# Decoding the packed weights on two engines: the low bits on GpSimd, the combining on VectorE

## The chip, the cores and the metric

The kernel runs on one core of a Trainium2 chip. The core has five engines with a queue of instructions each: TensorE (PE, matmuls), VectorE (DVE), ScalarE (ACT), GpSimd (POOL) and SyncE (SP, which here issues the loads and the transposes by DMA). The metric is the device time of one execution in microseconds, as the median of several runs; lower is better.

## The reference

Attention with a mask from hashed buckets, then a feed-forward layer with an ELU over its output:

```python
q_bits = (einsum('bhsd,dk->bhsk', q, proj) > 0)          # 6 bits a row, k the same
mask = q_bucket[:, :, :, None] == k_bucket[:, :, None, :]
scores = where(mask, q @ k.T / sqrt(D), -1e9)
attn = softmax(scores) ;  x = attn @ v                   # B 4, H 8, S 768, D 64
h = x @ w_in                                             # 3072 x 512 by 512 x 2048
g = where(h > 0, h, exp(min(h, 0)) - 1)
out = g @ w_out                                          # 3072 x 2048 by 2048 x 512
```

q, k, v and proj come as 32-bit numbers. The weights `w_in` and `w_out` come as 64-bit floating-point numbers, and the kernel reads them as pairs of 32-bit words.

## The kernel before, in words

**Work.** A batch has 8 heads, taken as 4 pairs. A chunk is a batch's rows that go through the feed-forward layer together: 2 x 128 tokens (three chunks) for the first batch, 3 x 128 (two chunks) for each other one. For each chunk and pair of heads the attention is done in steps called duos, each of two tiles of 128 rows: scores on PE (line 831), the row maximum while the scores leave PSUM on DVE (line 845), the exponential on ACT (line 869), then the normalised probabilities as two halves of 16 bits each, high part on ACT (`a_scaled`, line 238) and rest on DVE (`v_rest`, line 256), then a transpose by DMA (line 901) and the product with v on PE (line 924). When all four pairs of a chunk are done, its feed-forward matmuls can run (`h`, line 1002; `o`, line 1061), with the ELU between them on ACT, POOL (line 1027) and DVE (line 1030). Every matmul operand is split in this way into a high part and a rest of 16 bits, so each product is three matmuls.

**The weights.** `w_part` brings in 32 slabs of 128 x 512 weights, 16 of `w_in` and 16 of `w_out`. For each slab `load` (line 726) moves the 64-bit numbers into one of three places of a ring in the tile `U` (token `w`), or, for some of the slabs, into a spare place inside the tile `W` (token `raw`). Each number is a low and a high 32-bit word, next to each other. `prelu` on ACT (line 743) reads the high words and makes a 32-bit float from them whose last three bits have still to come. `shift` on DVE (line 747) shifts the dense slab left by three bits in place. `tail` on DVE (line 751) shifts the low words right by 29 and joins them in. Then the place in the ring is free again. `bound` on PE (line 762) sums the squares of the slab for the common scale. When 16 slabs are through, `scale` makes the scale of that matrix, and then each slab is split: `hi` on POOL (`scaled`, line 244) and `lo` on DVE (`v_rest`, line 256).

**The order.** Every step is a job with an engine, an estimated duration, a key (a due time counted in duos), the jobs it comes after, and tokens for buffers that it takes and gives back. `run_plan` simulates the engines with these estimates and with the constants at the head of the file (`HOP`, the delay from one engine to another; `BANK_HOP`, `LATE`, `LEAD`, `V_LEAD`, `W_KEY`, `OFF`), and emits the instructions in the order that it finds. On the chip each engine keeps the order of its own queue and waits where an input is not ready. `W_KEY` sets the keys of the weights: decoding at `W_KEY[0] + W_KEY[1] * i`, loads earlier by `W_KEY[2]` (a negative number: later), the splits of `w_in` from `W_KEY[3]` in steps of `W_KEY[4]`, those of `w_out` from `W_KEY[5]` in steps of `W_KEY[6]`. The jobs of the feed-forward layer on PE have keys over 1000, so PE takes them when nothing of the attention is due. `OFF` gives the key offset of each attention step. `GP` names the engine of some of the elementwise steps.

Of the kernel before, what the change touches and what calls it, by code (L numbers as in the profile page):

```python
# [49 lines left out]
GP = {'w': 'POOL', 'v0': 'ACT', 'v': 'POOL', 'k0': 'ACT', 'k': 'ACT', 'q0': 'POOL', 'q': 'ACT', 'kd': 'DVE', 'qd': 'DVE', 'kd0': 'POOL', 'qd0': 'DVE', 'ld': 'POOL', 'ld0': 'POOL'}  # L50
LATE_BITS = ()
FIRST = ((0,), (1,), (2,), (3,))
OUT = ("ACT", "DVE", "ACT")
OFF = {"S": -3.7, "M": -2.5, "N": 2.5, "E": 2.4, "R": -2.1, "H": 0.1, "L": -1.5, "A": 0.1}


@with_exitstack
def lsh_attention_moe(
# [10 lines left out]
    nc = tc.nc  # L69
# [459 lines left out]

    def bits_late(st, tag, key, after, w, quads, ways, dst, which):  # L530
        box = {}

        def mm():
            t = ps_a.tile([P, 512], F32, tag="av", name="z")[:, :w]
            box["t"] = t
            for n, (zi, src, rows) in enumerate(ways):
                for u in range(quads):
                    nc.tensor.matmul(  # L538
                        t[u * QD : (u + 1) * QD], pj["z"][:rows, zi, :], flat(st[src])[:rows, u * w : (u + 1) * w],
                        start=n == 0, stop=n == len(ways) - 1,  # L540
                    )

        def cmp():
            zb = small.tile([P, HALF], F16, tag="zb", name="zb", bufs=2)[:, :w]
            box["zb"] = zb
            used = slice(0, quads * QD)
            nc.vector.tensor_scalar(  # L547
                zb[used], box["t"][used], pj["thr"][used, which : which + 1], (MBIT, -MBIT)[which], ALU.is_gt, ALU.mult
            )

        def send():
            for u in range(quads):
                nc.sync.dma_start(flat(st[dst])[D : D + 2 * NB, u * w : (u + 1) * w], box["zb"][u * QD : u * QD + 2 * NB])

        m = job("PE", 0.08 + 0.22 * len(ways) * w / HALF, mm, key, after=after, take=("av",), kind="z")
        c = job("DVE", 0.13 + w * 0.00105, cmp, key, after=(m,), take=("zb",), give=("av",))
        return job("SP", 0.78 * quads, send, key, after=(c,), give=("zb",), move=0.1, lanes=quads)

    def q_split(ns, ps, nt, sgs, keys, early, made, klos):
        sts = [qs[n] for n in ns]  # L560
        w = len(ns)
        for i, (n, p, st, sg) in enumerate(zip(ns, ps, sts, sgs)):
# [19 lines left out]

            ky = keys[2] + (1.0 * i if not early else 0.0)
# [124 lines left out]
    def w_part():  # L708
        wst["acc"] = ps_o.tile([P, 512], F32, tag="o2", name="acc")[:, :SL]
        raw_users = []  # L710
        before = None
        decoded = {}
        scales = {}
        products = None
        for i in range(NSI + NSO):
# [28 lines left out]

            def shift(d=d):
                di = d.bitcast(I32)
                nc.vector.tensor_scalar(di, di, 3, None, ALU.logical_shift_left)  # L747

            def tail(i=i, d=d):
                di = d.bitcast(I32)  # L750
                nc.vector.scalar_tensor_tensor(di, w64.pop(i)[:, :, 0], 29, di, ALU.logical_shift_right, ALU.bitwise_or)  # L751

# [17 lines left out]
            if is_raw:  # L770
                raw_users.append(j3)
            decoded[i] = j3
            products = job("PE", 0.4, bound, key, after=(j3,), behind=(products,))
            if last:

                def scale(o=o):
                    nc.vector.tensor_reduce(wst["m2"][:, o : o + 1], wst["acc"], axis=AX.X, op=ALU.max)
                    wst["ex", o], wst["sc", o] = powers(
                        wst["m2"][:, o : o + 1], 1, 2.0**-34, W_TOP, f"w{o}", const, squares=True
                    )  # L780
                    if o == 1:
# [3 lines left out]
                scales[o] = products = job("DVE", 1.5, scale, key, after=(products,), take=("av",), give=("av",))  # L785
# [21 lines left out]
    def pair_part(n, ci, b, p, c0, nt, key0):  # L807
# [8 lines left out]
        for d, duo in enumerate(duos):  # L816
# [70 lines left out]
            for i, at in enumerate(duo):  # L887
# [300 lines left out]
```

## Time and profile before

| | |
|---|---|
| median of 3 runs | 886.24 us (885.35 to 886.65) |
| profiled execution: its own time | 886.83 us |
| profiled execution: span, first to last instruction | 884.7 us |
| mean granted TensorE clock | 0.964 |
| busy: PE, DVE, ACT, POOL | 804.8, 705.4, 664.6, 207.4 us |
| line 747, `shift`: count, mean | 32, 433 ns |
| line 751, `tail`: count, mean | 24 from the ring, 683 ns; 8 from `W`, 802 ns |
| line 743, `prelu`: count, mean | 24 and 8, 660 ns |

Busy time is the time in which an engine works on an instruction; waiting is not in it. A row of operations names the line, the engine, the operation, the tiles written and read, the shapes and the count, then the total and mean time. Where a line is that of a helper (238, 244, 256), the tiles tell the caller.

### The profile page before, as it was taken

How to read it: one execution, taken by the hardware profiler on the slowest of the kernel's cores; microseconds unless marked ns; L12 is line 12 of the kernel's file. 1: busy time of each engine (PE TensorE's matmuls, PEld its weight loads, DVE VectorE, ACT ScalarE, POOL GpSimd, SP SyncE). 2: the span in 40 equal slices, each digit the busy share in tenths (PEclk: the TensorE clock that was granted, in tenths of full speed). 3: DMA queues.
4: the chain of work that ended last, by engine and by line, in shares of the span. 5: the costliest groups of instructions: out<-in, count | busy, mean ns of one | idle time of the engine just before them, and what ended most of it. 6: DMA issues, size and time to landing. Idle time of an engine off the chain costs nothing.

```text
span 884.7 us, 15645 instructions
## 1 busy us (share of the span) xinstructions
PE 804.8 (91%) x5425; PEld 450.8 (51%) x5425; DVE 705.4 (80%) x1470; ACT 664.6 (75%) x1300; POOL 207.4 (23%) x268
## 2 busy tenths in 40 slices
PE   4666469999999987999999999999999999999996
PEld 2333246656666644555554555555555555555553
DVE  6999999999888777899796887898888868772321
ACT  7978457889697879987886888988778877862331
POOL 2100634422312101133131212142222112121211
PEclk9977579999999999999999999999999999999999
DMA  8588985999697889886897989987868786760000
GB/s 299 162 232 231 216 206 117 155 188 183 153 184 148 138 165 214 173 144 144 156 183 120 162 175 177 187 162 165 160 136 150 140 129 121 151 116 18 37 1 36
DMA packets 394927, 135.72 MB, mean 153 GB/s; under 512 B 370464, under 2 KB 389216, under 8 KB 394848
## 3 DMA queue, kind: packets, MB, share of 16 engines
q1 hardware_dynamic: 392768, 128.43, 72.1%
q0 software_dynamic: 1920, 6.29, 2.1%
q8 instruction: 42, 0.69, 0.3%
q14 instruction: 37, 0.30, 0.1%
q10 hardware_dynamic: 160, 0.00, 0.0%
HBM read 35.65 MB, written 6.29 MB: 47 GB/s over the span
## 4 chain that ended last, share of the span: by engine, by line
PE 62%; DVE 16%; issue 7%; ACT 5%; DMA 5%; SPq 2%; POOL 2%; POOLq 0%; DVEq 0%; ACTq 0%
PE o L1061 22%; PE h L1002 22%; PE ss L831 9%; PE av L924 7%; DVE hl L256 4%; DVE pt L845 4%; DVE W L256 1%; DVE W L751 1%; PE z L538 1%; ACT pt L869 1%; DVE U L1030 1%; DMA kst<-in_k_dram 1%; ACT hl L238 1%; DMA qst<-in_q_dram 1%; DVE W L747 1%
## 5 line engine op out<-in xcount | busy, mean ns | idle before, releaser
L1002 PE MATMUL h<-x,W 128*128 128x384 f16 (+1 forms) x1728 | 280.5, 309 | 1.1 <-DVE U L1030 1.1
L1061 PE MATMUL o<-W,U 128*128 128x512 f16 x1152 | 280.2, 383 | 0.4 <-ACT U L238 0.4
L256 DVE SCALAR_TENSOR_TENSOR hl<-pt,duo,hl 128x768 f16<-128x768 f32 x192 | 197.1, 1032 | 27.5 <-ACT hl L238 26.5
L1002 PEld LDWEIGHTS <-W 128*128 128x128 f16 x1728 | 167.1, 98 | 98.3 <-issue 7.7
L1027 POOL TENSOR_SCALAR U<-U,ch 128x384 f32<-128x384 f32 (+1 forms) x120 | 110.2, 918 | 434.6 <-ACT U L1023 316.6
L238 ACT ACTIVATE hl<-pt,duo 128x768 f16<-128x768 f32 x192 | 175.7, 925 | 33.5 <-DVE duo L882 28.4
L845 DVE TENSOR_SCALAR_CACHE_REDUCE pt<-ss 128x768 f32<-128x768 f32 x184 | 174.4, 948 | 32.7 <-PE ss L831 30.8
L869 ACT ACTIVATE pt<-pt,duo,sg 128x768 f32<-128x768 f32 x192 | 195.6, 1019 | 2.3
L1061 PEld LDWEIGHTS <-U 128*128 128x128 f16 x1152 | 111.4, 98 | 123.3 <-issue 9.0
L831 PE MATMUL ss<-K,O 128*128 128x384 f16 x736 | 154.6, 333 | 10.9 <-DVE pt L845 10.3
L831 PEld LDWEIGHTS <-O 128*128 128x128 f16 (+1 forms) x768 | 72.6, 100 | 78.1 <-issue 29.8
L924 PE MATMUL av<-PT,vhl 128*64 128x384 f16 (+1 forms) x1296 | 106.9, 322 | 5.1 <-DMA PT<-hl 3.2
L1023 ACT ACTIVATE U<-h,ch 128x384 f32<-128x384 f32 (+1 forms) x120 | 71.1, 592 | 49.1 <-PE h L1002 48.9
L238 ACT ACTIVATE U<-U,ch 128x384 f16<-128x384 f32 (+1 forms) x120 | 75.5, 629 | 38.8 <-PE o L1061 33.6
L1030 DVE SCALAR_TENSOR_TENSOR U<-h,U 128x384 f32<-128x384 f32 (+1 forms) x120 | 69.0, 575 | 41.3 <-POOL U L1027 41.2
L256 DVE SCALAR_TENSOR_TENSOR U<-U,ch 128x384 f16<-128x384 f32 (+1 forms) x120 | 77.6, 646 | 22.5 <-ACT U L238 22.1
L924 PEld LDWEIGHTS <-vhl 128*64 128x64 f16 x1296 | 74.3, 115 | 37.9 <-issue 12.0
L861 ACT ACTIVATE duo<-duo,sg 128x2 f32<-128x2 f32 x96 | 27.6, 287 | 30.0 <-DVE pt L845 29.6
L248 POOL COPY nat2q<-nat2q 128x192 f32<-128x192 f32 (+1 forms) x34 | 22.0, 646 | 119.2 <-DVE nat2q L256 84.5
L762 PE MATMUL acc<-W 128*128 128x128 bf16 x128 | 16.3, 264 | 27.2 <-DVE W L751 26.9
L869 ACT ACTIVATION_READ_ACCUMULATOR pt<-pt,duo,sg 128x1 f32 x192 | 36.0, 187 | 0.0
L547 DVE TENSOR_SCALAR zb<-z,pjt 64x384 f16<-64x384 f32 (+2 forms) x44 | 25.5, 579 | 6.5 <-PE z L538 6.1
(124 smaller groups left out, 571.0 us busy)
## 6 DMA issues: line engine op xcount, KB each, us to landing
U<-in_moe_w_in_dram SPq DMA_DIRECT2D x12, 512.0 KB
vf<-in_v_dram SPq DMA_DIRECT2D x16, 384.0 KB
U<-in_moe_w_out_dram SPq DMA_DIRECT2D x12, 512.0 KB
out_dram<-W POOLq DMA_DIRECT2D x24, 256.0 KB, 4.0
kst<-in_k_dram SPq DMA_DIRECT2D x14, 384.0 KB
qst<-in_q_dram SPq DMA_DIRECT2D x24, 192.0 KB
PT<-hl SPq DMA_TRANSPOSE x192
W<-in_moe_w_in_dram SPq DMA_DIRECT2D x4, 512.0 KB
```

The costliest lines, as they stand in the source:

```text
L238: nc.scalar.activation(o, x, AF.Copy, scale=s)
L256: nc.vector.scalar_tensor_tensor(o, x, s, hi, ALU.mult, ALU.subtract)
L831: nc.tensor.matmul(t[:, x, :HALF], st[o][:rows, at, :], kst[kk][:rows, j * NC + x * HC : j * NC + (x + 1) * HC, :].rearrange("p a b -> p ( ...
L845: nc.vector.tensor_scalar(pt.rearrange("p (n e) -> p n e", n=2), box["s", i][:, :, :HALF], CLAMP, None, ALU.max, ALU.max, accum_out=box["d ...
L861: nc.scalar.activation(u[:, 2:4], u[:, 0:2], AF.Copy, scale=st["sg"][:, 1:2])
L869: nc.scalar.activation(pt, pt, AF.Exp, bias=u[:, 2 + i : 3 + i], scale=st["sg"][:, 0:1], accum_out=u[:, 4 + i : 5 + i])
L924: nc.tensor.matmul(av[j * D : (j + 1) * D], vst["v"][p][:, j, c, vx, :], PTs[j][:, :nt, px, c, :], start=n_ == 0 and c == 0, stop=n_ == 2 ...
L1002: nc.tensor.matmul(box["h"][:, x * w : (x + 1) * w], WH[:, g * KT + t, wx, fc * P : (fc + 1) * P], xs[ns[t]][:, xx, :], start=x == 0 and t ...
L1023: nc.scalar.activation(box["e"], box["h"], AF.Exp, scale=css[b][:, 0:1])
L1027: nc.gpsimd.tensor_scalar(box["e"], box["e"], css[b][:, 2:3], css[b][:, 3:4], ALU.mult, ALU.add)
L1030: nc.vector.scalar_tensor_tensor(box["e"], box["h"], 0.0, box["e"], ALU.max, ALU.min)
L1061: nc.tensor.matmul(banks[bank][:, :DO], box["g"][:, gx, at : at + P], WH[:, NSI + f, wx, :], start=f == 0 and i == 0, stop=f == NF - 1 and ...
```

## The change

`prelu` stays. The new `shift` runs on GpSimd: it takes the low words as unsigned integers, multiplies them by 2^-29, takes the minimum with 7 and writes the result, rounded to an integer, over the low words. It no longer reads what `prelu` writes, so both wait for the load alone. `tail` on VectorE shifts the dense slab left by three bits and joins the low words in, in one instruction. It waits for `prelu` and for `shift`. The instruction on VectorE that only shifted is gone.

With it the plan gets new numbers: estimated durations of some steps, hops, leads, weight keys and offsets. The load of a slab into the ring is tied in the plan to the `tail` that frees its place.

```diff
-HOP = {"PE": 0.00, "ACT": 0.50, "DVE": 0.20, "POOL": 0.39, "SP": 0.49}
+HOP = {"PE": 0.00, "ACT": 0.50, "DVE": 0.20, "POOL": 0.20, "SP": 0.49}
-BANK_HOP = {"s0": 0.58, "s1": 0.58, "h": 0.00, "av": 0.00, "PT": 0.52, "hl": 1.44}
+BANK_HOP = {"s0": 0.58, "s1": 0.58, "h": 0.14, "av": 0.00, "PT": 0.52, "hl": 1.44}
-V_LEAD = (8.8, 7.7, 8.8, 2.9)
-V_LEAD0 = (-2.2, -1.0, 1.7, 1.5)
-W_KEY = (-4.6, 0.39, -1.3, 6.8, 0.20, 13.0, 0.33)
+V_LEAD = (7.4, 7.7, 8.8, 2.9)
+V_LEAD0 = (-2.2, -1.2, 4.4, 1.5)
+W_KEY = (-4.6, 0.39, -1.9, 5.8, 0.20, 14.4, 0.12)
-GP = {..., 'ld0': 'POOL'}
+GP = {..., 'ld0': 'POOL', 'sh': 'POOL'}
+WPE = 0
+JOINT = False
-OFF = {"S": -3.7, "M": -2.5, "N": 2.5, "E": 2.4, "R": -2.1, "H": 0.1, "L": -1.5, "A": 0.1}
+OFF = {"S": -3.2, "M": -2.5, "N": 2.5, "E": 2.5, "R": -2.1, "H": -0.6, "L": -1.5, "A": 0.1}
...
-            before = job("SP", 0.45, load, key - W_KEY[2], behind=(before,), take=ring, move=1.7)
+            last_use = staged[-3] if not is_raw and len(staged) > 2 else None
+            before = job("SP", 0.45, load, key - W_KEY[2], after=(last_use,), behind=(before,), take=ring, move=1.7)
...
-            def shift(d=d):
-                di = d.bitcast(I32)
-                nc.vector.tensor_scalar(di, di, 3, None, ALU.logical_shift_left)
+            apart = GP["sh"] == "POOL"
+
+            def shift(i=i, d=d):
+                if apart:
+                    low = w64[i][:, :, 0]
+                    nc.gpsimd.tensor_scalar(low, low.bitcast(U32), 2.0**-29, 7.0, ALU.mult, ALU.min)
...
             def tail(i=i, d=d):
                 di = d.bitcast(I32)
-                nc.vector.scalar_tensor_tensor(di, w64.pop(i)[:, :, 0], 29, di, ALU.logical_shift_right, ALU.bitwise_or)
+                low = w64.pop(i)[:, :, 0]
+                if apart:
+                    nc.vector.scalar_tensor_tensor(di, di, 3, low, ALU.logical_shift_left, ALU.bitwise_or)
...
             j1 = job("ACT", 0.56, prelu, key, after=wait)
-            j2 = job("DVE", 0.34, shift, key, after=(j1,))
-            j3 = job("DVE", 0.6, tail, key, after=(j2,), give=ring)
+            if apart:
+                j2 = job("POOL", 1.15, shift, key, after=wait)
...
+            j3 = job("DVE", 0.72 if is_raw else 0.62, tail, key, after=(j1, j2), give=ring)
...
-            w_ready[i] = job("DVE", 0.66, lo, key, after=(h,))
+            if i >= WPE:
+                w_ready[i] = job("DVE", 0.74, lo, key, after=(h,))
...
-                l = job("DVE", 0.93, lo, kd + OFF["L"], after=(h,), behind=los, give=("pt",) + (("duo",) if i == 1 else ()))
+                l = job("DVE", 0.95, lo, kd + OFF["L"], after=(h,), behind=los, give=("pt",) + (("duo",) if i == 1 else ()))
```

The plan's estimate for the copies of q on POOL (`dup`, `dup2`) becomes 0.6 + 0.35 nt for 0.2 + 0.15 nt. The diff also adds two options that are off: `JOINT`, one job for the hash bits of two pairs, and `WPE`, weight slabs whose rest is made by PE and ACT. With `JOINT = False` and `WPE = 0` neither issues an instruction.

More of the change, by code (lines that the diff above doesn't have):

```diff
@@ L13 @@
 I32 = mybir.dt.int32
+U32 = mybir.dt.uint32
 AF = mybir.ActivationFunctionType
@@ L45 @@
 LEAD0 = (-50.0, -3.9, -6.7, -1.8)
-V_LEAD = (8.8, 7.7, 8.8, 2.9)
-V_LEAD0 = (-2.2, -1.0, 1.7, 1.5)
-W_KEY = (-4.6, 0.39, -1.3, 6.8, 0.20, 13.0, 0.33)
+V_LEAD = (7.4, 7.7, 8.8, 2.9)
+V_LEAD0 = (-2.2, -1.2, 4.4, 1.5)
+W_KEY = (-4.6, 0.39, -1.9, 5.8, 0.20, 14.4, 0.12)
 S_LAG = 11
-GP = {'w': 'POOL', 'v0': 'ACT', 'v': 'POOL', 'k0': 'ACT', 'k': 'ACT', 'q0': 'POOL', 'q': 'ACT', 'kd': 'DVE', 'qd': 'DVE', 'kd0': 'POOL', 'qd0': 'DVE', 'ld': 'POOL', 'ld0': 'POOL'}
+GP = {'w': 'POOL', 'v0': 'ACT', 'v': 'POOL', 'k0': 'ACT', 'k': 'ACT', 'q0': 'POOL', 'q': 'ACT', 'kd': 'DVE', 'qd': 'DVE', 'kd0': 'POOL', 'qd0': 'DVE', 'ld': 'POOL', 'ld0': 'POOL', 'sh': 'POOL'}
 LATE_BITS = ()
+WPE = 0
+JOINT = False
 FIRST = ((0,), (1,), (2,), (3,))
 OUT = ("ACT", "DVE", "ACT")
-OFF = {"S": -3.7, "M": -2.5, "N": 2.5, "E": 2.4, "R": -2.1, "H": 0.1, "L": -1.5, "A": 0.1}
+OFF = {"S": -3.2, "M": -2.5, "N": 2.5, "E": 2.5, "R": -2.1, "H": -0.6, "L": -1.5, "A": 0.1}
 @with_exitstack
@@ L528, in bits_early, with bits_late @@
         return job("DVE", 0.12 + w * 0.00108, cmp, key, after=(m,), give=("h",))
-    def bits_late(st, tag, key, after, w, quads, ways, dst, which):
+    def bits_late(sts, key, after, w, each, ways, dst, which):
         box = {}
+        quads = each * len(sts)
         def mm():
@@ L538, in mm @@
                     nc.tensor.matmul(
-                        t[u * QD : (u + 1) * QD], pj["z"][:rows, zi, :], flat(st[src])[:rows, u * w : (u + 1) * w],
+                        t[u * QD : (u + 1) * QD], pj["z"][:rows, zi, :],
+                        flat(sts[u // each][src])[:rows, u % each * w : (u % each + 1) * w],
                         start=n == 0, stop=n == len(ways) - 1,
@@ L581, in alloc @@
                 )
-            ky = keys[2] + (1.0 * i if not early else 0.0)
+            ky = keys[2] + (1.0 * i if not early and not JOINT else 0.0)
             eng = GP["q0" if early else "q"]
@@ L633, in q_split @@
                     done.append(bits_early(st, "O1", "O2", ((2, P, 0), (2, P, 1)), a, w_, 1, kz, turned + proj_job))
+            elif early or not JOINT:
+                done = [bits_late([st], kz, turned + proj_job, nt * P, 2, ((2, "O1", P), (2, "O2", P)), "O2", 1)]
             else:
-                done = [bits_late(st, "O", kz, turned + proj_job, nt * P, 2, ((2, "O1", P), (2, "O2", P)), "O2", 1)]
+                done = []
             st["ready"] = done + turned
+        if not early and JOINT:
+            after = [j for st in sts for j in st["ready"]]
+            done = bits_late(sts, keys[3], after + proj_job, nt * P, 2, ((2, "O1", P), (2, "O2", P)), "O2", 1)
+            for st in sts:
+                st["ready"] = [done] + st["ready"]
     vs = {}
@@ L711, in w_part @@
         before = None
+        staged = []
         decoded = {}
@@ L767, in w_part @@
             j1 = job("ACT", 0.56, prelu, key, after=wait)
-            j2 = job("DVE", 0.34, shift, key, after=(j1,))
-            j3 = job("DVE", 0.6, tail, key, after=(j2,), give=ring)
-            if is_raw:
-                raw_users.append(j3)
+            if apart:
+                j2 = job("POOL", 1.15, shift, key, after=wait)
+            else:
+                j2 = job("DVE", 0.34, shift, key, after=(j1,))
+            j3 = job("DVE", 0.72 if is_raw else 0.62, tail, key, after=(j1, j2), give=ring)
+            (raw_users if is_raw else staged).append(j3)
             decoded[i] = j3
@@ L780, in scale @@
                     )
+                    if i < WPE:
+                        if "diag" not in wst:
+                            t = xp.tile([P, 2, HALF], F16, tag="x16", name="x16", bufs=2 * NP)
+                            t = t.rearrange("p a b -> p (a b)")
+                            wst["diag"] = [t[:, 2 * n * P : 2 * (n + 1) * P].bitcast(F32) for n in range(2)]
+                            wst["minus"] = t[:, 4 * P : 5 * P]
+                            nc.vector.tensor_scalar(wst["minus"], ident, -1.0, None, ALU.mult)
+                        nc.vector.tensor_scalar(wst["diag"][o], ident, wst["sc", o], None, ALU.mult)
                     if o == 1:
@@ L783, in scale @@
                         nc.vector.tensor_tensor(wst["e2"], wst["ex", 0], wst["ex", 1], ALU.mult)
-                scales[o] = products = job("DVE", 1.5, scale, key, after=(products,), take=("av",), give=("av",))
+                scales[o] = products = job("DVE", 1.5, scale, key, after=(products,), take=("av",) + (("x",) if o == 0 and WPE else ()), give=("av",))
         w_ready["scale"] = scales
@@ L799, in w_part, with rest, take_out @@
             h = job(GP["w"], hi_us(GP["w"], SL), hi, key, after=(scales[o], w_ready.get(i - 2)))
-            w_ready[i] = job("DVE", 0.66, lo, key, after=(h,))
+            if i >= WPE:
+                w_ready[i] = job("DVE", 0.74, lo, key, after=(h,))
+                continue
+            bank = {}
+            def rest(i=i, o=o, bank=bank):
+                bank["t"] = ps_h.tile([P, 512], F32, tag="h", name="rest")
+                nc.tensor.matmul(bank["t"], wst["diag"][o], W[:, i + 2, :], start=True, stop=False)
+                nc.tensor.matmul(bank["t"], wst["minus"], WH[:, i, 0, :], start=False, stop=True)
+            def take_out(i=i, bank=bank):
+                nc.scalar.activation(WH[:, i, 1, :], bank["t"], AF.Copy)
+            m = job("PE", 1.15, rest, key, after=(h,), take=("h",))
+            w_ready[i] = job("ACT", 0.61, take_out, key, after=(m,), give=("h",) + (("x",) if i == WPE - 1 else ()))
     xs = {}
```

16 lines of the change are left out of this document (11 added, 5 removed).

## The prediction

> **What bounds the kernel now.** I read the page first, then busy time by stretches, then the chain, then single operations.
>
> ```profile
> span 884.7 us, 15645 instructions
> PE 804.8 (91%) x5425; PEld 450.8 (51%) x5425; DVE 705.4 (80%) x1470; ACT 664.6 (75%) x1300; POOL 207.4 (23%) x268
> PE   4666469999999987999999999999999999999996
> DVE  6999999999888777899796887898888868772321
> ```
>
> The page's slices (22 us each, busy tenths) show two regimes: for six and a half slices DVE is full and PE at 4 to 6 tenths, then PE is full. The stretches give the sizes; columns are busy time by engine with instructions, PE's granted clock, DMA share, GB/s.
>
> ```profile
> core 0: us, PE busy (x) PEld busy (x) DVE busy (x) ACT busy (x) POOL busy (x), PEclk, DMA share, GB/s
> 0.00:20.00 20.00, 7.67 (x40) 3.83 (x40) 12.14 (x49) 14.26 (x27) 5.93 (x30) 1.00 0.91 316
> 20.00:72.00 52.00, 32.53 (x231) 17.18 (x231) 50.32 (x111) 43.21 (x85) 4.74 (x6) 0.87 0.72 197
> 72.00:125.00 53.00, 28.84 (x199) 16.85 (x200) 50.83 (x105) 32.84 (x67) 22.71 (x19) 0.65 0.94 233
> 125.00:145.00 20.00, 17.96 (x164) 13.70 (x163) 18.80 (x47) 13.72 (x29) 4.88 (x6) 0.92 0.49 97
> 145.00:884.70 739.70, 717.84 (x4796) 399.20 (x4794) 573.31 (x1161) 560.55 (x1096) 169.10 (x208) 0.99 0.74 142
> 320.00:340.00 20.00, 14.47 (x73) 6.18 (x70) 16.35 (x37) 16.07 (x33) 2.20 (x4) 0.83 0.93 177
> ```
>
> Behind 145 us PE idles 739.70 - 717.84 = 21.9 us, 5.5 of them in the hole at 320 to 340. Ahead of 145 it idles 145 - (7.67 + 32.53 + 28.84 + 17.96) = 58.0 us. In 20 to 145 us DVE is busy 50.32 + 50.83 + 18.80 = 119.95 of 125 us (96%): in this opening DVE sets the pace, and PE, though its granted clock is down to 0.65, does not. What brings the full stretch forward brings the end forward, since the work behind is the same. The chain of waits for 20 to 145 us, and for its two main parts (20 to 72, 72 to 125), says what the opening consists of:
>
> ```profile
> by line: issue 12.7%; DVE pt L845 11.8%; DVE W L751 9.1%; DVE hl L256 8.7%; DVE W L747 5.7%; DVE W L256 5.4%; DMA U<-in_moe_w_in_dram 4.4%; POOL nat2q L248 3.9%; ACT W L743 3.4%; ACT pt L869 3.2%; PE h L1002 3.2%; DMA W<-in_moe_w_in_dram 3.
> by line: issue 10.8%; DMA U<-in_moe_w_in_dram 10.5%; DVE pt L845 10.2%; DVE W L751 10.0%; ACT W L743 8.1%; DVE hl L256 7.9%; ACT pt L869 7.8%; DMA W<-in_moe_w_in_dram 7.6%; DVE W L747 5.4%; ACT hl L238 3.2%; ACT vhl L238 2.9%; DVE O L522 2.
> by line: issue 16.3%; DVE pt L845 12.9%; DVE hl L256 10.9%; DVE W L751 10.4%; POOL nat2q L248 9.3%; DVE W L256 8.6%; DVE W L747 8.3%; POOL W L244 7.0%; DVE vhl L256 4.1%; ACT hl L238 3.3%; DVE zb L547 1.6%; DVE nat2q L256 1.5%; DVE x L942 1
> ```
>
> The shift that leaves (L747) is 5.7% of 125 us = 7.1 us of that chain. First the operations of DVE in 20 to 145 us by line (busy us, mean ns), then minimum/median/maximum in ns:
>
> ```profile
> L256 DVE SCALAR_TENSOR_TENSOR hl<-pt,duo,hl 128x768 f16<-128x768 f32 x22 | 23.0, 1047 | 0.0
> L256 DVE SCALAR_TENSOR_TENSOR W<-W,w0s 128x512 f16<-128x512 f32 x16 | 12.9, 821 | 2.0 <-POOL W L244 2.0
> L747 DVE TENSOR_SCALAR W<-W 128x512 int32<-128x512 int32 x30 | 12.9, 434 | 0.1
> L751 DVE SCALAR_TENSOR_TENSOR W<-W 128x512 int32<-128x512 int32 x7 | 5.5, 790 | 0.1
> L256 DVE SCALAR_TENSOR_TENSOR vhl<-vf,vs,vhl 128x384 f16<-128x384 f32 x8 | 5.2, 661 | 0.0
> ```
>
> ```profile
> L747 DVE TENSOR_SCALAR W<-W x32: 408/420/773, 13.9 to 128.7; 128x512 int32<-128x512 int32 x32
> L751 DVE SCALAR_TENSOR_TENSOR W<-U,W x24: 671/684/693, 19.3 to 131.2; 128x512 int32<-128x512 int32 x24
> L751 DVE SCALAR_TENSOR_TENSOR W<-W x8: 671/690/1061, 14.3 to 123.7; 128x512 int32<-128x512 int32 x8
> L256 DVE SCALAR_TENSOR_TENSOR hl<-pt,duo,hl x22: 1004/1009/1441, 42.7 to 142.0; 128x768 f16<-128x768 f32 x22
> L256 DVE SCALAR_TENSOR_TENSOR W<-W,w0s x16: 724/740/1172, 92.5 to 137.6; 128x512 f16<-128x512 f32 x16
> L256 DVE SCALAR_TENSOR_TENSOR vhl<-vf,vs,vhl x8: 604/606/1040, 62.5 to 100.3; 128x384 f16<-128x384 f32 x8
> ```
>
> POOL's nearest rows, and ACT's step that runs beside the new one:
>
> ```profile
> L244 POOL TENSOR_SCALAR W<-W,w0s 128x512 f16<-128x512 f32 x16 | 16.8, 1055 | 34.4 <-DVE w0s L279 23.2 <-DVE W L256 11.2
> L244 POOL TENSOR_SCALAR W<-W,w0s x16: 684/1023/1974, 72.4 to 123.5; 128x512 f16<-128x512 f32 x16
> L248 POOL COPY nat2q<-nat2q x5: 289/746/4926, 42.9 to 133.3; 128x128 f32<-128x128 f32 x5
> L743 ACT ACTIVATE W<-U x24: 642/660/684, 16.0 to 125.4; 128x512 f32<-128x512 f32 x24
> ```
>
> Equal instructions spread widely on both engines: a POOL copy of 289 ns took 4926 once, and DVE rows of 1009, 740, 606 ns reach 1441, 1172, 1040. The two engines hold each other up, so moving work between them has a price on both sides.
>
> **The change part by part.** *The shift leaves DVE.* 32 instructions, 30 of them in the 125 us: 30 x 434 ns = 13.0 us of DVE.
>
> *The combining instruction stays.* It still reads the strided low word and the dense slab, 512 elements of 4 bytes: 684 ns as now. I take no change. Ends: -0.4 us (all at the minimum of 671, 32 x 13 ns) and +3.4 us (all at the 790 mean of the raw-buffer form, 32 x 106 ns).
>
> *POOL gets 32 instructions* on 512 strided words, integer to integer through a multiplication and a minimum. No row has that form. Nearest is POOL's scaling of a dense slab of 512: 684 ns at least, 1055 mean, 1974 at most. I take the mean, since the new ones run among the same DVE work: 33.8 us; ends 21.9 and 63.2 us. POOL is idle 47.3 us in 20 to 72 and 30.3 in 72 to 125, so the 16 of w_in in the first part and the 16 of w_out in the second (16.9 us each) fit. At 1974 each the second part needs 31.6 us, more than its idle time. The new instruction sits in POOL's queue in order and waits for a weight load; behind it wait the scalings of the weights (L244) and the copies of q (L248), and for those DVE and PE.
>
> *Collisions on DVE.* Mean less median in the rows above: hl 22 x 38 ns, W 16 x 81, vhl 8 x 55, shift 30 x 14, raw combining 7 x 100 = 0.84 + 1.30 + 0.44 + 0.42 + 0.70 = 3.7 us, beside 6 + 19 + 6 = 31 POOL instructions in these 125 us: 0.12 us each. For 32 more: 3.8 us. Ends: 0 (most rows are at their median) and 0.43 us each (the worst, 1441 - 1009 and 1172 - 740), 13.8 us.
>
> *From load to combined slab.* Now ACT 660, then DVE 420; after it ACT 660 beside POOL 1055. 1080 against 1055: where the load comes last, nothing changes. Ends: by 684, 0.4 us less a slab; by 1974, 0.9 us more, 14 us if all 16 slabs of one part met it in series. The zero rests on ACT's 660 and on the other work in DVE's queue, which lies over the rest.
>
> *Loads and SP.* A load is now held in the plan until the third last staged slab is combined, and its key moves 0.6 later; SP's queue moves loads past transposes of the probabilities (L901).
>
> ```profile
> SPq L726 <- DVE W L751: 30.4, 12, 6.9
> ACT W L743 <- DMA W<-in_moe_w_out_dram: 5.9, 2, 5.5
> ACT W L743 <- DMA U<-in_moe_w_out_dram: 3.4, 4, 1.2
> PE av L924 <- DMA PT<-hl: 3.2, 1, 3.2
> ```
>
> (Total us, times, longest.) SP stood 30.4 us before loads until a slab was combined, with transposes behind it; PE waited once for a transpose, 3.2 us; ACT waited 9.3 us for late loads. So the ends are -3.2 and +9.3 us. I take 0: earlier transposes against later loads.
>
> *New planner numbers everywhere.* Hops, leads and offsets of the attention steps change; the split of w_in (16 scalings on POOL, 16 rests on DVE) is due 1.0 key unit earlier, that of w_out starts 1.4 later and goes faster, 0.12 a slab for 0.33. The splits issue no DMA; on POOL they move past copies of q and the ELU's step (L1027), on DVE past pair steps. Nothing is added or removed by it, but all queues are reordered. Bounds: behind 145 us at best PE's 21.9 us of idle time go; at worst another hole as the one of 5.5 us opens per misplaced step. I take 0, and for the range one such hole either way.
>
> **The sum.** DVE is relieved of 13.0 - 3.8 = 9.2 us in a stretch that it fills to 96%: 8.8 us if all of it arrives. The chain allows 7.1. I take 7.1, the shift's share, since chain time not on DVE (issue 12.7%, loads 4.4%, POOL copies 3.9%) does not shrink with it. What is late next is the weight load in 20 to 72 and POOL's queue in 72 to 125. The profiled execution took 886.83 us by its own time, 2.1 above its span and 0.59 above the median of 886.24. 886.24 - 7.1 = 879.1 us.
>
> **Rivals.**
> *1. The stall on DVE eats the gain, and more (slower).* Place: 20 to 125 us, DVE instructions with two slabs as inputs. One POOL instruction takes the place of one shift, so it decides from the shift's own 0.43 us of hold-up per new instruction: just the worst rows. If each new one holds DVE for its own whole undisturbed 684 ns, DVE loses 32 x 684 = 21.9 us for 32 x 434 = 13.9 gained: +8.0 us, 894 us. For it: DVE at 96% leaves few free moments. Against: the mean is 0.12, and DVE's reductions out of PSUM (L845, 11.8% of the chain) leave POOL room.
> The Trainium skill, "SBUF — State Buffer", section Who interferes with whom, states this rule: a GpSimd instruction and a DVE one in a 2-port mode or with two SBUF inputs share one port pair, whoever starts first holds it for the whole instruction and the other blocks. By that rule taken at its fullest the time is this rival's 894, against 879 by the rows; the trace agrees that POOL is shut out (4926 for 289) but shows no hold-up of DVE as long as a whole POOL slab instruction, 0.43 at most.
>
> *2. The second part yields nothing.* From 1.89 us per new instruction ((53 - 22.71) / 16) POOL is full in 72 to 125, or DMA (share 0.94 there already) does not deliver sooner. Only the 5.4% of 52 us = 2.8 us from the first part remain: 883.4 us. For it: the rows of 1974 and 4926 lie in this part. Against: PE and ACT wait little for DMA there.
>
> *3. The new order opens a hole.* One as at 320 to 340 costs 5.5: 884.6 us, no measurable change; two and more: 890 and up. As likely the other way, a hole closes: 879.1 - 5.5 = 873.6, and with no collisions (3.8) 869.8.
>
> *4. It does not do what it says:* the combining waits for POOL where it waited for the shift. With 8 slabs that meet the 1974 in series, 8 x (1974 - 1080) = 7.2 us, all the gain is gone: 886.
>
> **How the numbers follow.** Forecast 879 (875 to 882): 0.48. Hole closed or no collisions, about 873: 0.10. Rival 2, 883.4: 0.13. One hole or rival 4, 885 to 886: 0.11. Rival 1 at 894: 0.11. Several holes, 890: 0.07. A measurement of this kernel tells 0.2% (1.8 us) from no change: faster 0.71, same 0.11, slower 0.18. The range 870 to 890 goes from the 869.8 of a closed hole without collisions to several holes, and leaves out rival 1 and what lies beyond these, some 0.16. The likeliest alone has 875 to 882: without collisions 3.8 less, with the dearer combining 3.4 more.
>
> **What would show it.** L747 gone from DVE; DVE's busy time down by some 10 us to 695; POOL's up by 30 to 38 to about 241, the new instruction at about 1.05 us; first MoE matmul and the full PE stretch some 7 us earlier; PE's idle time behind that near 22 us. Wrong, if the new POOL instruction has a median over 1.9 us, if DVE's rows for hl and W rise by over 0.2 us in the mean, if ACT or PE wait longer for weight loads, or if PE's idle time behind 145 us moves by over 5 us.

## The result: slower by 1.1%, and the profile after

The changed kernel takes 896.50 us (median of 4 runs, 894.19 to 897.43), the kernel before 886.44 on the same chip: ratio 1.0107, 95% interval 1.0083 to 1.0132. The forecast was 879.1, in a range of 870 to 890. The profiled execution took 896.37 us by its own time, with a span of 894.6.

The page of the kernel after, with the same lines that were shown of before:

```profile
span 894.6 us, 15683 instructions
PE 812.6 (91%) x5425; PEld 457.3 (51%) x5425; DVE 702.2 (78%) x1438; ACT 667.2 (75%) x1300; POOL 277.7 (31%) x300
PE   4775358999999997999999999999999999999996
DVE  6899879999889777898799887898877888752331
POOL 5876774532322111232041112232321111111211
```

POOL's row of before, for comparison:

```profile
POOL 2100634422312101133131212142222112121211
```

DVE lost 3.2 us of busy time where ten were forecast, POOL gained 70.3 where 30 to 38 were, and POOL is at 5 to 8 tenths in the first six slices, where it was at 0 to 6. The stretches of after (busy us by engine, PE's clock, DMA share, GB/s), and behind them the first 145 us of before:

```profile
core 0: us, PE busy (x) PEld busy (x) DVE busy (x) ACT busy (x) POOL busy (x), PEclk, DMA share, GB/s
20.00:72.00 52.00, 35.54 (x226) 20.35 (x226) 48.86 (x96) 42.53 (x84) 39.34 (x24) 0.76 0.74 201
72.00:125.00 53.00, 25.16 (x164) 14.94 (x165) 43.77 (x88) 27.94 (x57) 41.26 (x27) 0.56 0.78 181
125.00:145.00 20.00, 15.75 (x126) 10.35 (x125) 16.93 (x46) 13.79 (x30) 10.43 (x8) 0.80 0.77 179
0.00:145.00 145.00, 84.54 (x554) 49.65 (x555) 122.27 (x275) 98.65 (x195) 102.48 (x91) 0.73 0.78 208
145.00:894.60 749.60, 728.03 (x4873) 407.67 (x4870) 579.92 (x1165) 568.54 (x1106) 175.23 (x210) 0.99 0.74 141
```

```profile
0.00:145.00 145.00, 87.00 (x631) 51.55 (x632) 132.09 (x310) 104.04 (x205) 38.26 (x61) 0.81 0.80 212
```

Behind 145 us PE idles 749.60 - 728.03 = 21.6 us; before it was 21.9. So nothing was lost there: the whole loss comes from the opening. By 145 us PE did less (554 matmuls at a granted clock of 0.73, for 631 at 0.81), and 728.03 - 717.84 = 10.2 us more of its work are left over, at the same clock of 0.99. DVE is busy 48.86 + 43.77 + 16.93 = 109.56 of the 125 us where it was busy 119.95: it was relieved, and it waits. What the lower clock by itself cost was not tested; DVE waited for PE 2.9 us in these 125 us, 1.6 before. In 72 to 125 us POOL's busy time went from 22.71 to 41.26. The first matmul of the feed-forward layer, in the timeline of before and of after, starts 9.2 us later:

```profile
125.15 1.48 PE L1002 MATMUL h<-x,W 128*128 128x256 f16 x6
```

```profile
134.37 0.83 PE L1053 MATMUL h<-x,W 128*128 128x256 f16 x6
```

What POOL does there: the new instruction (line 766), first its total in us and its mean, then minimum/median/maximum in ns; then who waited in 20 to 145 us (us, times, longest), and the chain of the same stretch:

```profile
L766 POOL TENSOR_SCALAR U<-U 128x512 int32<-128x512 uint32 x24 | 53.5, 2229 | 6.6 <-DMA U<-in_moe_w_out_dram 3.6 <-DMA U<-in_moe_w_in_dram 0.6 <-DVE qs L416 0.5
L766 POOL TENSOR_SCALAR W<-W 128x512 int32<-128x512 uint32 x8 | 16.9, 2108 | 4.7 <-DMA W<-in_moe_w_in_dram 4.3
```

```profile
L766 POOL TENSOR_SCALAR U<-U x24: 1976/2144/2694, 13.2 to 135.6; 128x512 int32<-128x512 uint32 x24
L766 POOL TENSOR_SCALAR W<-W x8: 1976/2052/2492, 10.0 to 120.6; 128x512 int32<-128x512 uint32 x8
```

```profile
POOL W L247 <- DVE W L259: 9.0, 4, 5.0
DVE W L775 <- POOL U L766: 6.8, 8, 1.9
DVE W L775 <- POOL W L766: 1.6, 2, 0.8
```

```profile
by line: issue 14.0%; POOL U L766 11.2%; DVE hl L259 10.5%; DVE pt L896 9.5%; DVE W L775 8.6%; POOL W L247 5.8%; DVE W L259 4.7%; POOL W L766 3.6%; DVE vhl L259 3.4%; ACT W L758 2.6%; ACT pt L920 2.4%; PE ss L882 2.1%; ACT vhl L241 2.0%; DV
```

No instance of the new instruction is shorter than 1976 ns; the forecast had 1055. It is 11.2 + 3.6 = 14.8% of 125 us = 18.5 us of the chain, where the shift that it replaced was 7.1. DVE's combining (line 775) waits for it.

### The profile page after: what moved, and what is told of

Read it like the earlier page. It is cut to its first block, busy times and chain, and to the rows that moved or that the text cites. A ratio compares the mean times of both kernels' runs of the same rounds, so it can differ in the third digit from the quotient of the medians.

```text
span 894.6 us, 15683 instructions
## 1 busy us (share of the span) xinstructions
PE 812.6 (91%) x5425; PEld 457.3 (51%) x5425; DVE 702.2 (78%) x1438; ACT 667.2 (75%) x1300; POOL 277.7 (31%) x300
## 4 chain that ended last, share of the span: by engine, by line
PE 61%; DVE 17%; issue 7%; DMA 5%; POOL 4%; ACT 4%; SPq 1%; POOLq 0%; DVEq 0%; ACTq 0%
PE h L1053 21%; PE o L1112 21%; PE ss L882 10%; PE av L975 8%; DVE hl L259 4%; DVE pt L896 3%; DMA PT<-hl 2%; DVE W L259 2%; POOL U L766 2%; DVE W L775 1%; PE z L542 1%; DMA qst<-in_q_dram 1%; ACT pt L920 1%; POOL W L247 1%; DVE U L259 1%
## 5 line engine op out<-in xcount | busy, mean ns | idle before, releaser
L1078 POOL TENSOR_SCALAR U<-U,ch 128x384 f32<-128x384 f32 (+1 forms) x120 | 113.7, 948 | 418.7 <-ACT U L1074 336.2
L882 PE MATMUL ss<-K,O 128*128 128x384 f16 x736 | 157.5, 338 | 17.8 <-DVE pt L896 17.8
L975 PE MATMUL av<-PT,vhl 128*64 128x384 f16 (+1 forms) x1296 | 108.8, 324 | 3.6 <-DMA PT<-hl 3.0
L975 PEld LDWEIGHTS <-vhl 128*64 128x64 f16 x1296 | 76.7, 116 | 36.6 <-issue 16.7
L259 DVE SCALAR_TENSOR_TENSOR U<-U,ch 128x384 f16<-128x384 f32 (+1 forms) x120 | 78.1, 651 | 20.8 <-ACT U L241 20.1
L766 POOL TENSOR_SCALAR U<-U 128x512 int32<-128x512 uint32 x24 | 53.5, 2229 | 6.6 <-DMA U<-in_moe_w_out_dram 3.6
L251 POOL COPY nat2q<-nat2q 128x192 f32<-128x192 f32 (+1 forms) x34 | 19.1, 563 | 94.7 <-DVE nat2q L259 67.6
```

What stands on the lines that cost most here:

```text
L259: nc.vector.scalar_tensor_tensor(o, x, s, hi, ALU.mult, ALU.subtract)
L766: nc.gpsimd.tensor_scalar(low, low.bitcast(U32), 2.0**-29, 7.0, ALU.mult, ALU.min)
L882: nc.tensor.matmul(t[:, x, :HALF], st[o][:rows, at, :], kst[kk][:rows, j * NC + x * HC : j * NC + (x + 1) * HC, :].rearrange("p a b -> p ( ...
L975: nc.tensor.matmul(av[j * D : (j + 1) * D], vst["v"][p][:, j, c, vx, :], PTs[j][:, :nt, px, c, :], start=n_ == 0 and c == 0, stop=n_ == 2 ...
L1078: nc.gpsimd.tensor_scalar(box["e"], box["e"], css[b][:, 2:3], css[b][:, 3:4], ALU.mult, ALU.add)
```

## The experiments

All ratios are to runs of the kernel before on the same chip (medians 887.8 to 888.4 there). Three theories stood at the start: (1) the new instruction's length, (2) the new order from the new planner numbers, (3) hold-ups of DVE by GpSimd.

**Instructions and planner numbers apart.** First the new numbers with the old instructions, then the old numbers with the new instructions.

```diff
# old_ops_new_plan, against the kernel after
-GP = {..., 'sh': 'POOL'}
+GP = {..., 'sh': 'DVE'}
# new_ops_old_plan, against the kernel before
-            def shift(d=d): ... nc.vector.tensor_scalar(di, di, 3, None, ALU.logical_shift_left)
+            def shift(i=i): ... nc.gpsimd.tensor_scalar(low, low.bitcast(uint32), 2.0**-29, 7.0, ALU.mult, ALU.min)
-                nc.vector.scalar_tensor_tensor(di, low, 29, di, ALU.logical_shift_right, ALU.bitwise_or)
+                nc.vector.scalar_tensor_tensor(di, di, 3, low, ALU.logical_shift_left, ALU.bitwise_or)
-            j2 = job("DVE", 0.34, shift, key, after=(j1,))
-            j3 = job("DVE", 0.6, tail, key, after=(j2,), give=ring)
+            j2 = job("POOL", 1.15, shift, key, after=wait)
+            j3 = job("DVE", 0.6, tail, key, after=(j1, j2), give=ring)
```

> The changed kernel's planner numbers with the old two instructions of VectorE (shift, then combine); nothing new on GpSimd. Theory 1, the new GpSimd instruction's own length (2.0 us and more against the 1.05 I had assumed) costs the time: back near the kernel before, 883 to 889 us. Theory 2, the new order of the queues costs it: it stays at 893 to 898 us. Theory 3, VectorE is held up by GpSimd's accesses: as theory 1.

> The kernel before, planner numbers kept, with the new instructions alone: GpSimd makes the low bits (estimated at 1.15 us in the plan as in the change), VectorE combines in one step. Theory 1 and theory 3: slower than before by about as much as the change, 894 to 900 us. Theory 2: faster than before, 876 to 883 us.

Measured: 912.84 us, 1.0277 (1.0257 to 1.0298), and 902.97 us, 1.0168 (1.0145 to 1.0191). The second is slower than before, as theories 1 and 3 have it, though 3 us beyond their 894 to 900. The first fits none: the new numbers alone, with the old instructions, are worse than the whole change. With the old instructions the numbers cost 2.8%; with the new ones they gain 0.6% (1.0168 to 1.0107). In the first kernel PE idles 38.0 us behind 145 us, for 21.9 before, which is 16 of the 25.8 us that the span is longer. Two rows (a stretch, and PE's waits behind 145 us), of that kernel and then of before, show part of it: a hole of 13.3 us at 300 to 360 us (before 7.2), and PE waiting 19.8 us for DVE's reductions to free the score banks (before 6.7).

```profile
300.00:360.00 60.00, 46.71 (x296) 24.62 (x294) 44.60 (x102) 47.83 (x93) 5.78 (x9) 0.85 0.90 176
PE ss L882 <- DVE pt L896: 19.8, 17, 2.8
```

```profile
300.00:360.00 60.00, 52.81 (x340) 28.37 (x335) 45.63 (x91) 48.66 (x96) 8.12 (x12) 0.94 0.93 179
PE ss L831 <- DVE pt L845: 6.7, 9, 2.5
```

**The same order, a shorter instruction.**

```diff
# half_width and quarter_width (128 for 256), against the kernel after
-                    low = w64[i][:, :, 0]
+                    low = w64[i][:, :256, 0]
...
-                    nc.vector.scalar_tensor_tensor(di, di, 3, low, ...)
+                    nc.vector.scalar_tensor_tensor(di as 2 x 256, di, 3, low repeated 2 times, ...)
```

> The changed kernel, instruction for instruction in the same order on every engine, but GpSimd works on half of each slab's low words (256 of 512), and the combining instruction reads these twice; half of the weights so get another weight's last three bits. The new GpSimd instruction should take about 1.05 us, the duration that my prediction had assumed. Theory 1: the loss is gone and the predicted gain appears, 878 to 885 us. Theory 2: still 893 to 897 us. Theory 3 (each GpSimd instruction holds VectorE once, whatever its length): most of the loss stays, 890 to 895 us, with the mean of VectorE's hl row in 20 to 145 us as high as in the change.

> As the half-width kernel, but GpSimd works on 128 of each slab's 512 low words (about 0.55 us), and the combining reads them four times; three quarters of the weights get another weight's last three bits. If the instruction's length sets the time: below the half width's, 877 to 883 us. If the number of GpSimd instructions does: the same as the half width, 883 to 886 us.

Measured: 884.57 us, 0.9944 (0.9925 to 0.9963), and 881.17 us, 0.9929 (0.9914 to 0.9945). Both kernels leave out low words, and so show the time alone. With the new instruction at 1.09 us at least and 1.24 in the median (1.06 was assumed), or at 0.65 and 0.66, the change is a gain, in its own order on every queue. Theory 2 falls for the change itself, and theory 3 in the form "once for each instruction, whatever its length".

**Why is the instruction so long?** Forms of it, alone on the chip behind the kernel's end.

```diff
+        g(s0 as int32, s0 as uint32, 2.0**-29, 7.0, ALU.mult, ALU.min)      # 1221: stride 8 bytes
+        g(dense1, dense1, 2.0**-29, 7.0, ALU.mult, ALU.min)                 # 1224: dense, 32-bit float
+        nc.scalar.activation(s0 as int32, s0 as uint32, AF.Copy, scale=2.0**-29)   # 1230
...
```

> The changed kernel with eleven forms of the 512-element instruction, two of each, behind its end, where nothing else runs; only the rows of these count. If the conversion of integers is what makes the new instruction long, then the form from 32-bit float to 32-bit float with the same stride takes 0.7 to 0.8 us and the dense integer form about 2.0. If the stride of 8 bytes does, the dense integer form takes about 0.7 and the strided float form about 2.0. ScalarE should take about 0.66 for the same words, VectorE 0.35 to 0.65.

Rows of single lines (minimum/median/maximum):

```profile
L1221 POOL TENSOR_SCALAR U<-U x2: 1959/1962/1965, 890.2 to 915.2; 128x512 int32<-128x512 uint32 x2
L1224 POOL TENSOR_SCALAR U<-U x2: 1917/1917/1917, 896.2 to 910.4; 128x512 f32<-128x512 f32 x2
L1230 ACT ACTIVATE U<-U x2: 651/651/651, 914.0 to 926.9; 128x512 int32<-128x512 uint32 x2
```

Both guesses fall: neither stride nor conversion matters by more than 0.05 us. A dense float to float form takes 1917 ns. The kernel's own scalings, 684 ns at least, are two multiplications; the nine slow forms are a multiplication and a minimum in eight cases (1917 to 1965 ns) and one multiplication alone in the ninth (1533 to 1538). So the next forms vary the operations:

```diff
+        g(s0 as int32, s0 as uint32, 2.0**-29, 1.0, ALU.mult, ALU.mult)   # 1221
+        g(dense1, dense1, 0.5, 1.0, ALU.mult, ALU.mult)                   # 1225
+        g(dense1, dense1, 0.5, 1.0, ALU.mult, ALU.max)                    # 1227
+        g(dense1, dense1, 0.5, None, ALU.mult)                            # 1229
...
```

> The changed kernel with twelve more forms on GpSimd behind its end, two of each, alone on the chip; only their rows count. Theory A: two multiplications, or a multiplication and an addition, take 0.68 to 0.8 us on 512 elements in every type and stride; those with a minimum or maximum 1.9 us. Theory B: forms with an integer input or output stay at 1.5 us and over.

```profile
L1221 POOL TENSOR_SCALAR U<-U x2: 631/634/638, 890.0 to 903.4; 128x512 int32<-128x512 uint32 x2
L1225 POOL TENSOR_SCALAR U<-U x2: 617/620/622, 891.3 to 902.7; 128x512 f32<-128x512 f32 x2
L1227 POOL TENSOR_SCALAR U<-U x2: 1922/1924/1927, 894.1 to 906.7; 128x512 f32<-128x512 f32 x2
L1229 POOL TENSOR_SCALAR U<-U x2: 1496/1498/1501, 898.1 to 910.7; 128x512 f32<-128x512 f32 x2
```

Theory A holds, with 0.62 to 0.64 us for the fast pairs where it had 0.68 to 0.8: two multiplications take 0.63 us with the integers and the stride of the change, a minimum or maximum makes it 1.92 to 1.96, and, not expected by any theory, one multiplication alone takes 1.50 on dense floats.

**The change's own order, the fast form.** 7.49 / 2^32 as the factor makes the minimum needless, since no word can then round to more than 7. It is not quite the same function: with the smaller factor some of the three-bit numbers come out one lower.

```diff
# mult_mult, against the kernel after; mm_old_plan makes the same edit in new_ops_old_plan
-                    nc.gpsimd.tensor_scalar(low, low.bitcast(U32), 2.0**-29, 7.0, ALU.mult, ALU.min)
+                    nc.gpsimd.tensor_scalar(low, low.bitcast(U32), 7.49 * 2.0**-32, 1.0, ALU.mult, ALU.mult)
```

> The changed kernel with one thing other: GpSimd's new instruction multiplies by 7.49 / 2^32 and then by 1.0 instead of by 2^-29 and taking the minimum with 7 (the top then rounds to 7 by itself). Every queue has the same instructions in the same order. Theory A, the minimum makes the instruction slow (kernel's own scalings, two multiplications on 512 elements, take 0.68 us; every form with a multiplication and a minimum took 1.92 to 1.96 alone, whatever stride and type): the new instruction takes 0.7 to 0.8 us alone and the time is 876 to 884 us, 0.5 to 1.2% faster than before. Theory B, integers in or out are slow too: 1.5 to 2.0 us and 890 to 897 us.

> The kernel of the new instructions under the old planner numbers, with the same order on every engine, but two multiplications in the place of multiplication and minimum. Under the new numbers this edit was worth 1.0107 to 0.9984 of the time before, 10.9 us. If the instruction's length is the cost in any order: 903 goes down by 8 to 13 us to 890 to 895 us. If that was a chance of the new order: 898 to 904 us.

Measured: 886.95 us, 0.9984 (0.9971 to 0.9997), and 890.82 us, 1.0036 (1.0021 to 1.0051). In both orders the length alone costs about the same: 1.0107 - 0.9984 = 1.2%, 10.9 us, and 1.0168 - 1.0036 = 1.3%. The second lies in the range for a cost in any order. The first lies in neither range of its own: the forecast gain of 0.8% does not come, 0.16% does. Compared with the quarter-width kernel, in which the instruction is about as short, 4.9 us are missing. The rows of the two, of the half width and of after, in 20 to 72 us for DVE's `hl`:

```profile
L766 POOL TENSOR_SCALAR U<-U x24: 638/732/1323, 13.1 to 127.1; 128x512 int32<-128x512 uint32 x24
L259 DVE SCALAR_TENSOR_TENSOR hl<-pt,duo,hl x7: 1005/1051/1485, 41.1 to 70.3; 128x768 f16<-128x768 f32 x7
```

```profile
L766 POOL TENSOR_SCALAR U<-U x24: 650/659/1312, 13.1 to 120.1; 128x128 int32<-128x128 uint32 x24
L259 DVE SCALAR_TENSOR_TENSOR hl<-pt,duo,hl x8: 1005/1018/1133, 39.7 to 67.7; 128x768 f16<-128x768 f32 x8
```

```profile
L766 POOL TENSOR_SCALAR U<-U x24: 1092/1242/1767, 13.9 to 124.0; 128x256 int32<-128x256 uint32 x24
L259 DVE SCALAR_TENSOR_TENSOR hl<-pt,duo,hl x8: 1007/1018/1161, 39.4 to 68.0; 128x768 f16<-128x768 f32 x8
```

```profile
L259 DVE SCALAR_TENSOR_TENSOR hl<-pt,duo,hl x8: 1005/1015/1392, 41.5 to 71.1; 128x768 f16<-128x768 f32 x8
```

The worst `hl` is 0.47 us over 1.01 with two multiplications on 512 words (0.64 us long), 0.38 with multiplication and minimum on 512 (1.98 us), 0.15 on 256, 0.12 on 128. The longest hold-up goes with the number of words that GpSimd handles, not with the length of its instruction. It is one instance a kernel, and the sum of the hold-ups is another matter: the same 512 words cost DVE more in all with the short form than with the long one (8.0 against 6.1 us, worked out below). Why is not shown.

**No access by GpSimd, same order.** The low bits on ScalarE, at the same place of the emission, so that the orders of PE, DVE and SP are unchanged; and the same edit with the plan told (ScalarE, 0.56 us), so that the order is made anew, under both sets of numbers.

```diff
# act_same_order, against the kernel after (its plan still counts a GpSimd job)
-                    nc.gpsimd.tensor_scalar(low, low.bitcast(U32), 2.0**-29, 7.0, ALU.mult, ALU.min)
+                    nc.scalar.activation(low, low.bitcast(U32), AF.Copy, scale=7.49 * 2.0**-32)
# act_new_plan: besides; act_old_plan: both in new_ops_old_plan
-                j2 = job("POOL", 1.15, shift, key, after=wait)
+                j2 = job("ACT", 0.56, shift, key, after=wait)
```

> The changed kernel's own order, unchanged on PE, VectorE and SyncE; the 32 low-bit instructions leave GpSimd's queue and stand in ScalarE's queue at the same place of the emission. No bit of the result is left out. Port theory: with two multiplications on GpSimd the time was 886.9 us with 12.0 us of hold-ups of VectorE in 20 to 145 us against 4.3 before; with ScalarE the hold-ups go back to under 5 and the time to 878 to 883 us, as in the quarter-width kernel (881.2), where they were 4.8. If ScalarE, with 32 x 0.65 = 21 us more in the opening, becomes the limit: 887 to 895 us.

> The new planner numbers, and the low bits made by ScalarE (0.65 us alone for these words) in the place of GpSimd; the plan is told 0.56 us on ScalarE, so the order is another. Theory port (GpSimd's reads hold up VectorE's instructions with two slabs as inputs): VectorE's excess in 20 to 145 us falls from 8.6 (change) and 12.0 us (two multiplications) to under 5, its hl row's mean from 1157 to under 1060 ns. The time, if the order is no worse than the change's: 878 to 888 us; if ScalarE becomes the limit of the opening (it has 41 us free in 145, the 32 need 21): 888 to 900.

> The same with ScalarE under the old planner numbers. Port theory: as above for VectorE's rows. Time 878 to 888 us if the relief of VectorE by 13 us arrives; over 888 if the order under the old numbers, made for the old instructions, does not fit the new ones.

Measured: act_same_order 883.37 us, 0.9954 (0.9939 to 0.9968); act_new_plan 894.76 us, 1.0079 (1.0062 to 1.0096); act_old_plan 895.62 us, 1.0087 (1.0066 to 1.0108). The first beats the kernel before and the change with no low word left out; it is 0.4 us over the range of the port theory. Its stretches:

```profile
0.00:145.00 145.00, 93.08 (x653) 56.77 (x654) 127.70 (x292) 124.37 (x245) 37.84 (x63) 0.80 0.85 217
145.00:881.00 736.00, 715.55 (x4774) 400.13 (x4772) 569.34 (x1149) 558.54 (x1088) 172.11 (x205) 0.99 0.74 142
```

PE does 653 matmuls by 145 us, where it did 631 before and 554 after. In the other two VectorE is relieved as well (the excess that the expectations name is down to some 5 us; `hl`'s mean is 1053 ns in act_old_plan, but 1087 in act_new_plan, where the held-up instances lie beside GpSimd's scalings), but the new order has a hole at 300 to 360 us. The time of act_new_plan lies in the range for ScalarE as the limit of the opening, yet the opening is not what is longer: PE has 681 matmuls done by 145 us, and idles 30.3 us behind it, for 20.5 in act_same_order. This is the stretch in act_new_plan (60 - 45.32 = 14.7 us idle; before 7.2, after 8.8, act_same_order 8.0):

```profile
300.00:360.00 60.00, 45.32 (x266) 22.45 (x265) 41.21 (x89) 48.22 (x96) 4.32 (x8) 0.83 0.90 174
```

**Other orders.** The plan told the true length of the change's instruction (2.15); of the two multiplications (0.73); and only w_in's slabs decoded in the new way, under the old numbers.

```diff
# honest_plan: kernel after, 2.15; mm_told: mult_mult, 0.73
-                j2 = job("POOL", 1.15, shift, key, after=wait)
+                j2 = job("POOL", 2.15, shift, key, after=wait)
# mm_w_in_only: mm_old_plan with the old two instructions of DVE for i >= NSI
+            j2 = job("POOL", 0.75, ...) if i < NSI else job("DVE", 0.34, shift, key, after=(j1,))
```

> The changed kernel with the plan's estimate of the new GpSimd instruction at 2.15 us for 1.15, as measured. If the loss came from an order that was made for a short instruction: 880 to 890 us. If it comes from the instruction's length itself, which no order removes while GpSimd stands 80% busy in 20 to 125 us: 892 to 900 us.

> The two multiplications on GpSimd with the plan's estimate at the measured 0.73 us for 1.15, so every queue is ordered anew. If a right estimate makes a better order: 878 to 885 us. If the orders scatter by themselves, whatever the estimate (the honest estimate of 2.15 for the change gave 911): anywhere from 885 to 912 us, with PE's idle time at 300 to 360 us, 8.8 in the change, as the mark of it.

> Old planner numbers; the 16 slabs of w_in get the new instructions (two multiplications on GpSimd, one combining step), those of w_out the old two of VectorE. GpSimd was idle 47 us in 20 to 72 us before, and its scalings of w_in come later. If the hold-up of VectorE is per GpSimd instruction and most of the price of the second half is the queue behind the scalings: 880 to 886 us. If the order decides more than the instructions: outside of 878 to 890.

Measured: 911.45 us, 1.0263 (1.0243 to 1.0283); 891.39 us, 1.0050 (1.0031 to 1.0070); 895.06 us, 1.0071 (1.0045 to 1.0097). Telling the plan the truth made it worse in both cases: honest_plan lies beyond every expectation, and mm_told, in which only the estimate differs from mult_mult, costs 0.7% more, within the range that scatter was given. The orders scatter by more than 1% with the same instructions. Half of the change under the old numbers brought no gain either: its 895 us is outside of 878 to 890, where the order decides more than the instructions. The hole at 300 to 360 us explains part: honest_plan has 19.6 us of it (60 - 40.40). In mm_told the mark that the expectation named fails, 7.0 us idle there; PE idles 26.9 us behind 145 us for 20.8 in mult_mult, in other places. Which planner number opens a hole was not tried.

## Why the prediction was wrong, step by step

*The shift leaves DVE, the combining stays.* Right: line 747 is gone, and the combining takes 673 at least and 692 in the median, for 671 and 684.

*POOL's 32 instructions.* This step failed. The forecast took the nearest row by shape, the scaling of a slab, at its mean of 1055 ns: 33.8 us. They took 53.5 + 16.9 = 70.4 us, mean 2229 and 2108, and 1976 at least. Even the upper end, 1974, a scaling that was itself held up, lies below the shortest instance. The row was of the same engine, shape and element size, but of another pair of operations, and that set the length: 0.63 against 1.96 us on the same words. Its price, measured in the change's own order, is 10.9 us (1.2%), more than the whole loss of 1.07%. The first sign of being wrong that the forecast named, a median over 1.9 us, came (2144 and 2052 ns).

*Collisions on DVE.* Right in kind, and near in size for the change itself. In the forecast's own measure, mean less undisturbed median over `hl`, W, `vhl` and the two combining forms in 20 to 145 us (medians of before), the hold-ups are 3.3 us before, 6.1 after, 8.0 with two multiplications, 4.4 and 3.3 at half and quarter width, 3.6 with ScalarE. For the change that is 21 x 100 + 16 x 104 + 8 x 105 + 23 x 28 + 7 x 125 ns from the first five rows, for two multiplications 22 x 148 + 16 x 52 + 8 x 190 + 23 x 58 + 7 x 145 ns from the other five:

```profile
L259 DVE SCALAR_TENSOR_TENSOR hl<-pt,duo,hl 128x768 f16<-128x768 f32 x21 | 23.3, 1109 | 1.1 <-ACT hl L241 1.0
L775 DVE SCALAR_TENSOR_TENSOR W<-W,U 128x512 int32<-128x512 int32 x23 | 16.1, 712 | 6.9 <-POOL U L766 6.8
L259 DVE SCALAR_TENSOR_TENSOR W<-W,w0s 128x512 f16<-128x512 f32 x16 | 13.3, 844 | 1.6 <-POOL W L247 1.6
L775 DVE SCALAR_TENSOR_TENSOR W<-W 128x512 int32<-128x512 int32 x7 | 5.7, 815 | 1.7 <-POOL W L766 1.6
L259 DVE SCALAR_TENSOR_TENSOR vhl<-vf,vs,vhl 128x384 f16<-128x384 f32 x8 | 5.7, 711 | 0.0
```

```profile
L259 DVE SCALAR_TENSOR_TENSOR hl<-pt,duo,hl 128x768 f16<-128x768 f32 x22 | 25.5, 1157 | 1.1 <-DMA U<-in_moe_w_out_dram 1.0
L775 DVE SCALAR_TENSOR_TENSOR W<-W,U 128x512 int32<-128x512 int32 x23 | 16.7, 742 | 0.3 <-POOL U L766 0.2
L259 DVE SCALAR_TENSOR_TENSOR W<-W,w0s 128x512 f16<-128x512 f32 x16 | 12.4, 792 | 1.6 <-POOL W L247 1.6
L259 DVE SCALAR_TENSOR_TENSOR vhl<-vf,vs,vhl 128x384 f16<-128x384 f32 x8 | 6.4, 796 | 0.0
L775 DVE SCALAR_TENSOR_TENSOR W<-W 128x512 int32<-128x512 int32 x7 | 5.8, 835 | 0.0
```

The forecast had 3.8 us more than before; it was 2.8 for the change and 4.7 with two multiplications. Counted over every form of DVE's instructions, each against its own median, it was some 4 us more for the change and some 8 with two multiplications. Removing them from the fast form was worth 0.3% (0.9984 to 0.9954 with ScalarE, which pays 21 us of its own) to 0.55% (0.9929 at quarter width), 2.7 to 4.9 us.

*From load to combined slab.* Forecast at zero. DVE waited 6.8 + 1.6 = 8.4 us for line 766 in the 125 us, and 0.2 with two multiplications: rival 4's mechanism, from the length.

*Loads and SP.* Forecast at 0, and nothing was lost there: in 20 to 145 us ACT waited 4.0 us for late loads of `w_out`, for 9.3, and PE's one wait of 3.2 us for a transpose is gone.

*Planner numbers.* Forecast at 0, with one hole of 5.5 us either way. For the change itself that was near: -0.6% under the slow form, -0.5% under the fast one (1.0036 to 0.9984). As a bound on what such numbers can do it was far off: +2.8% with the old instructions.

*The sum.* With a short instruction and few hold-ups the sum was nearly right: forecast -0.8%, half width -0.6%, quarter width -0.7%. The mechanism, DVE's relief in the opening, was right, and a POOL term at half its size turned the sign.

*The rivals.* Rival 1's 894 us is near the result by luck: hold-ups cost some 3 to 5 us where they were largest, not the 21.9 us of DVE's time that it counts. Of rival 2 the condition was met (over 1.89 us for each instruction), though POOL was busy 41.26 of the 53 us in 72 to 125 and not full. It was priced at 883.4, as a gain that does not come, where a long instruction delays what waits for it and stands behind it. In the change's own order the last scaling of `w_in` starts at 125.1 us, for 119.8 with two multiplications, and the first feed-forward matmul at 134.37, for 129.59. The scalings alone are not shown to be the path: against before the last one starts 1.6 us later, and that matmul comes 9.2 later, beside the `x` of the fourth pair of heads, which is 8.5 later (133.57 us for 125.04).

Two rules of the Trainium skill can be set beside this. "SBUF — State Buffer", section Who interferes with whom, has GpSimd and a VectorE instruction with two SBUF inputs exclude each other for the whole instruction. The runs agree that they hold each other up, but not that it lasts for the whole GpSimd instruction: one of 1.98 us held VectorE up no longer than one of 0.64 (0.38 and 0.47 at most in `hl` in 20 to 72 us). "GPSIMD Engine Reference", section 3.1, gives 1.8 cycles an element, 769 ns for 512 elements, as the best case of a tight elementwise loop; here the same 512 took 617 to 645, 1488 to 1538 or 1917 to 1965 ns, by the operations alone.

## What to carry to other kernels

Price an instruction that moves to GpSimd by a row with the same pair of operations, not only the same shape; if there is none, measure the form by itself first, and look for an equivalent one, as here a factor that makes a clamp needless. When work leaves a full VectorE for GpSimd, count the words that GpSimd will touch while VectorE is busy, since it holds VectorE up (3.3 us before, 6.1 to 8.0 with the 32 new instructions); ScalarE did the work without that. In a kernel whose queues are ordered by a plan, compare an edit in one fixed order, since a new order alone moved this kernel by 0.5 to 2.8%.

## What the runs showed of the hardware that was not expected

On GpSimd, on 512 elements in each partition: two multiplications, or a multiplication and an addition, 0.62 to 0.64 us; one multiplication or one minimum alone, 1.49 to 1.54; a multiplication with a minimum or maximum, 1.92 to 1.96. Stride (4 or 8 bytes) and type (32-bit float, signed, unsigned) changed this by under 0.05 us. So a second, idle multiplication by 1.0 makes an instruction faster. ScalarE scales 512 strided unsigned words and writes them as integers in 0.65 us; VectorE does it with the minimum in 0.43.
